# A cached-attention decode block on one core: the first and the last unit move into VectorE's and ScalarE's loops

## The chip, the core and the metric

The kernel runs on one core of one Trainium2 chip. The core has a matrix engine (TensorE, PE in the profile), a vector engine (VectorE, DVE), a scalar engine (ScalarE, ACT), GpSimd (POOL) and SyncE (SP), and 16 DMA engines that carry data between device memory and the on-chip memory. Each of the five engines runs its own list of instructions in order; they wait for one another through semaphores. In this kernel nearly all transfers are issued from SP, in one list and in order; ACT issues the first small input and the output.

The metric is device time in microseconds (us) of one execution. The kernel before takes 1277.06 us, the median of three runs (1276.95 to 1277.29).

## The reference, cut to what is computed

```python
B, Sq, D = 4, 1, 512
H, Sk, Dh = 32, 8192, 128
F = 1792

def _A_ref(x, k_cache, v_cache, wq, wo):
    q = (x @ wq).reshape(B, Sq, H, Dh).transpose(0, 2, 1, 3)
    scores = jnp.einsum("bhqd,bhkd->bhqk", q, k_cache) * (Dh ** -0.5)
    p = _softmax(scores, axis=-1)
    o = jnp.einsum("bhqk,bhkd->bhqd", p, v_cache)
    return o.transpose(0, 2, 1, 3).reshape(B, Sq, H * Dh) @ wo

def _B_ref(x, w_gate, w_up, w_down):
    return (_sigmoid(x @ w_gate) * (x @ w_up)) @ w_down

h = x + _A_ref(_layernorm(x), k_cache, v_cache, wq, wo)
return h + _B_ref(_layernorm(h), w_gate, w_up, w_down)
```

All inputs are bfloat16. The two caches are 4 x 32 x 8192 x 128 each, 268 MB each; the weights together are some 14 MB. One token per batch entry is decoded, so every cache byte is used once.

## The kernel before, in words

**Units.** The 128 pairs of batch entry and head are worked on four at a time: `NU` = 32 units. A unit has a K tile and a V tile, each 128 partitions x 64 KB (8 MB in all). The big tensor `KV` has `NSL` = 3 slots of that size: K of unit u goes to slot u % 2, V to slot 2 (the last V to slot 0). `KV` is declared at L172, after `kT`, `PTz`, `Lq`, `headw`, `q_all` (L170) and `spare` (L171; nothing reads or writes it), and its place in each partition follows from their sizes.

**The transfers** (L532 to L557, all on SP's list): Wq; then K0, K1, V0, K2, V1, K3 and so on in alternation (`order`); then Wo, Wgate, Wup and three pieces of Wdown. From the fourth tile on each K waits until unit u-2 has been read (`t_kd`, set by a small DVE memset at L361 behind the last transposition of a unit), and each V until the V tile before it has been used (`t_vd`, the first of four small matmuls at L415). V0 waits for the projection of q, which has read Wq out of slot 2.

**A unit** (`unit(u)`, L422) emits, in this order:
- `scores(u)`: 16 times, DVE transposes 128 x 1024 words of K into one half of `kT` (L335) and PE multiplies it with q (L344). `Lq` is a zeroed tensor in which `q_window(u)` (L328, DVE) puts the four queries of the unit, read from `q_all`.
- `maxima(u)`: DVE takes the row maximum (L361 to L367), ACT the exponential (L369).
- `q_window(u + 1)`, or in the last unit a memset of a dummy (L428).
- `pv(u - 1)`, not in unit 0: DVE's reciprocal of the sum of weights (L396), PE's 64 matmuls with V (L405), ACT's scaled copy to `O_sb` (L410; `O_sb` lies in the second half of `kT`), and the four small matmuls (L415), whose last token is `t_ex`.
- `weights(u)`: four DVE transpositions of the exponentials (L375), which wait for `t_ex` of the unit before, and a PE matmul that adds them up (L379, `t_sum`).

So DVE's order within a unit is 16 transpositions, the maxima, the next query window, the reciprocal, and the weights' transpositions.

**The lists and loops.** `_Prog` collects one list of steps for each engine. `open`, `begin`, `end` and `close` turn a part of a list into a loop on the chip: each turn is written out and must equal the first, and the loop runs it as often as there were turns. Semaphore counts go back to their start with each turn (`_rebase`, L67). Before, unit 0 is written out straight on all engines; PE then loops over units 1 to 31, one unit a turn; DVE and ACT loop over units 1 to 30, two units a turn (15 turns), and run unit 31 straight again. Behind the loop come twelve turns of `filler` matmuls on PE, `pv(31)`, the projection with Wo, the second layernorm and the gated unit, and the output.

Of the kernel before, what the change touches and what calls it, by code (L numbers as in the profile page):

```python
# [6 lines left out]
BF16 = mybir.dt.bfloat16  # L7
FP32 = mybir.dt.float32
ALU = mybir.AluOpType
# [9 lines left out]
class _Prog:  # L19
# [52 lines left out]
    def emit(self, eng, fn, waits=(), incs=1, ch=None):  # L72
        todo = self._waits(eng, waits)
        key = ch or eng
        tok = self.token(key, incs) if incs else None
        self._put(eng, todo, key, fn, incs, 1)
        return tok
# [41 lines left out]
def bass_sequential_preLN__mha_block_cached__glu_gated_glu__decode_kernel(  # L119
# [12 lines left out]
    B, _sq, D = A_x.shape  # L132
# [7 lines left out]
    NU = B * H // HU  # L140
# [4 lines left out]
    NT = R * DH // 2 // TW  # L145
# [8 lines left out]
    prog = _Prog({"p2d": "dve", "d2d": "dve", "a2d": "dve", "d2p": "pe", "a2p": "pe",  # L154
                  "d2a": "act", "p2a": "act",
                  "k0": "dve", "k1": "dve", "v2": "pe"})
    emit = prog.emit

    with ExitStack() as es:
        def SB(name, shape, dt):  # L160
            return es.enter_context(nc.sbuf_tensor(name, shape, dt))

        def raw(t):
            return t.tensor if hasattr(t, "tensor") else t
# [2 lines left out]
        PTz = SB("PTz", [128, 2048], BF16)  # L167
        Lq = SB("Lq", [128, 528], BF16)
        headw = SB("headw", [128, 128], FP32)
        q_all = SB("q_all", [128, NU, 4], BF16)  # L170
        spare = SB("spare", [128, 24], FP32)  # L171
        KV = SB("KV", [128, NSL * SLOT], BF16)  # L172
        E_sb = SB("E_sb", [128, 512], BF16)
# [3 lines left out]
        part = SB("part", [128, 32], FP32)  # L177
# [5 lines left out]
        dummy = SB("dumm", [128, 4], FP32)  # L183
# [32 lines left out]
        bank = [PS[:, 512 * i:512 * (i + 1)] for i in range(8)]  # L216
        SBK, OBK, EX, XS, XO, QB, DN = 0, 1, 2, 3, 4, (5, 6), 7
# [4 lines left out]
        for k in keys:  # L222
# [3 lines left out]
        slots = {(x, u): (0 if u == NU - 1 else 2) if x == "v" else u % 2 for x, u in order}  # L226
        toks = {x: prog.token(x[0] + str(slots[x]), 16) for x in order}
# [18 lines left out]
        t_mask = emit("pool", lambda e: e.affine_select(  # L246
            out=m42, in_=m42, compare_op=ALU.is_ge, fill=0.0, base=31,
            pattern=[[32, 4], [0, 2]], channel_multiplier=-1), [t0])
        t_lq0 = emit("pool", lambda e: e.memset(Lq[:, :], 0.0))
        t0 = emit("pool", lambda e: e.memset(lane[:, :], 0.0))  # L250
        for j in range(4):
# [9 lines left out]
        t_selc = emit("pool", lambda e: e.affine_select(  # L261
            out=hw4, in_=hw4, compare_op=ALU.is_ge, fill=0.0, base=31,
            pattern=[[0, 8], [32, 4], [0, 4]], channel_multiplier=-1), [t0])
        emit("pool", lambda e: e.memset(part[:, :], 1.0))
        t_pool = emit("pool", lambda e: e.memset(PTz[:, :], 0.0))
        for b in (OBK, EX, *QB, DN):
            t_ps0 = emit("act", lambda e, b=b: e.activation(bank[b], bass.AP(raw(Lq), 0, [[528, 128], [0, 512]]), ACT.Copy), [t_lq0])

        def cols(t, c):
            return t[:, c:c + NC * (B - 1) + 1:NC]  # L270
# [24 lines left out]
        for g in range(2):  # L295
            def f(e, g=g):
                made = []
                for c in range(NC):
                    for h in range(HU):
                        rhs = wq_v[:, c, 2048 * g:2048 * (g + 1)].rearrange("p (k h d) -> p h k d", k=4, h=HU)[:, h]  # L300
                        made.append(e.matmul(PS[32 * h:32 * h + B, 512 * QB[g]:512 * QB[g] + 512], cols(xnT, c), rhs,  # L301
                                             start=(c == 0), stop=(c == NC - 1), tile_position=(0, 32 * h)))
                return made[-4:]
# [3 lines left out]
            dst = qt[:, 512 * g:512 * (g + 1)].rearrange("p (k r w) -> p r k w", k=8, r=2)  # L307
            t_qr.append(emit("dve", lambda e, src=src, dst=dst: e.transpose(dst, src), [t_qp]))
        t_q = emit("dve", lambda e: e.tensor_copy(
            q_all[:, :, :].rearrange("p (b g) t -> p g b t", b=B),  # L310
            qt.rearrange("p (g t w) -> p g w t", t=4, g=NU // B)[:, :, 0:B, :]), t_qr)

        t_tr, t_sc, t_pv, t_ex, t_mx, t_exp, t_ptz, t_lq, t_ocp, t_rs, t_kd, t_vd, t_sum = ({} for _ in range(13))
        TU = 2
# [3 lines left out]
        def at(ix, d):  # L318
            return ix[d] if len(ix) > d else 0
# [5 lines left out]
        def q_window(u, t=0):  # L325
            dst = bass.AP(raw(Lq), 15, [[528, 128], [128, 4], [16, 8]])
            msk = bass.AP(raw(mask), 0, [[8, 128], [0, 4], [1, 8]])
            t_lq[u] = emit("dve", lambda e, ix: e.tensor_tensor(  # L328
                dst, bass.AP(raw(q_all), at(ix, 0) * (4 * TU) + 4 * (u - TU * t), [[NU * 4, 128], [1, 4], [0, 8]]), msk, ALU.mult),
                           [t_q, t_lq0, t_mask, t_sc.get((u - 1, NT - 1))], ch="d2p")  # L330

        def k_chunk(u, c):
            o = slots["k", u] * (SLOT // 2) + (NT - 1 - c) * TW
# [15 lines left out]
        def scores(u):  # L349
            clear(SBK, [t_lq[u], t_pool, t_ps0, t_selc])  # L350
            prog.open("pe")
            for c in range(NT):
                if c % 2 == 0:
                    prog.begin("pe")
                k_chunk(u, c)
                if c % 2:
                    prog.end("pe")
            prog.close("pe")
# [23 lines left out]
        def filler(n, turns=1):  # L382
            if turns > 1:
                prog.open("pe")
            for _ in range(turns):
                if turns > 1:
                    prog.begin("pe")
                emit("pe", lambda e: [e.matmul(bank[XS], Lq[:, 0:128], Lq[:, 0:512], start=True, stop=True) for _ in range(n)][-1],  # L388
                     [t_ps0, t_lq[NU - 1]], incs=0)
                if turns > 1:  # L390
                    prog.end("pe")
            if turns > 1:
                prog.close("pe")

        def pv(u, t):
            t_rs[u] = emit("dve", lambda e: e.reciprocal(rsb[:, :], bank[QB[1]][:, 1:2]), [t_sum[u]], ch="d2a")  # L396
            slot = slots["v", u]
            ob = 512 * OBK

            def f(e, ks):  # L400
                made = []
                for k in ks:
                    j, n, r4 = k % 4, k // 4, k % 4
                    lhsT = PTz[:, 512 * r4 + n:512 * r4 + n + 481:32]
                    made.append(e.matmul(PS[32 * j:32 * j + 16, ob:ob + 512], lhsT,  # L405
                                         KV[:, slot * SLOT + 512 * k:slot * SLOT + 512 * (k + 1)],
                                         start=(k < 4), stop=(k >= 60), tile_position=(0, 32 * j)))
                return made[-4:]
            t_pv[u] = emit("pe", lambda e: f(e, range(64)), [toks["v", u], t_ps0], incs=4, ch="p2a")
            t_ocp[u] = emit("act", lambda e: e.activation(O_sb, bank[OBK], ACT.Copy, scale=rsb[:, 0:1]), [t_pv[u], t_rs[u]], ch="a2p")  # L410

            def fs(e, ix, qs):
                ins = None
                for q in qs:
                    ins = e.matmul(bass.AP(raw(PS), at(ix, 0) * 4 + (512 * EX + 4 * (u - t)), [[4096, 128], [1, 4]]),  # L415
                                   O_sb[:, 128 * q:128 * (q + 1)], lane[:, q:q + 13:4],
                                   start=False, stop=(u == NU - 1 and q == 3), skip_group_check=True)
                return ins
            t_vd[u] = emit("pe", lambda e, ix: fs(e, ix, (0,)), [t_ocp[u], t_selc, t_ps0], ch="p2x")
            t_ex[u] = emit("pe", lambda e, ix: fs(e, ix, (1, 2, 3)), ch="p2d")  # L420

        def unit(u, t=0):  # L422
            scores(u)
            maxima(u)
            if u + 1 < NU:
                q_window(u + 1, t)
            else:
                emit("dve", lambda e: e.memset(dummy[:, 3:4], 0.0), ch="d2p")  # L428
            if u:
                pv(u - 1, u - 1)  # L430
            weights(u)

        emit("pe", lambda e: e.matmul(bank[EX][:, 0:128], PTz[:, 0:128], PTz[:, 0:128], start=True, stop=False,
                                      skip_group_check=True), [t_pool, t_ps0], incs=0)
        q_window(0)
        unit(0)

        prog.open("pe", "dve", "act")
        for u in range(1, NU):
            t, first = divmod(u - 1, TU)  # L440
            if u == NU - 1:
                prog.close("dve", "act")
                t = 0
            elif not first:
                prog.begin("dve", "act")
            prog.begin("pe")
            unit(u, t)
            prog.end("pe")
            if first:
                prog.end("dve", "act")  # L450
        prog.close("pe")
        filler(2, 12)
        pv(NU - 1, 0)
        t_oa = emit("dve", lambda e: e.tensor_tensor(  # L454
# [79 lines left out]
        for n, (x, u) in enumerate(order):  # L534
# [3 lines left out]
            slot = slots[x, u]  # L538
# [53 lines left out]
```

## Time and profile before

| | |
|---|---|
| median of three runs | 1277.06 us (1276.95 to 1277.29) |
| the profiled execution, its own time | 1276.83 us |
| its span, first to last instruction | 1275.6 us |
| busy: PE | 779.7 us |
| busy: DVE | 762.3 us |
| busy: ACT | 59.0 us |
| bytes moved by DMA | 550.83 MB |

The profile covers one execution. The span is what the trace covers; 1.2 us of the execution's own time lie outside it. Busy times are sums over an engine's instructions. The timeline's rows give the start from the span's beginning, the duration, the engine, the line of the kernel, the operation, what it writes and reads, and in brackets how long the engine was idle before and what ended that. A row for SPq or ACTq is the issue of a transfer; its landing shows in the instruction that waited for it. Queue rows count packets, megabytes and the time that the packets took as a share of the time of all 16 DMA engines.

### The profile page before, as it was taken

Reading aid. Unit: us, or ns where it says so; the run is one execution under the profiler, and the core shown is the slowest. Engines: PE = TensorE matmul, PEld = TensorE weight load, DVE = VectorE, ACT = ScalarE, POOL = GpSimd, SP = SyncE. Lnnn points to the kernel's source line nnn. Section 1 sums busy time; section 2 is a strip of 40 time slices with the busy share of each in tenths; the row PEclk is TensorE's granted clock in tenths of the full one; section 3 lists DMA queues with packets and bytes.
Section 4 is the critical chain, followed back from the end, with each engine's and each line's share of the span. In section 5 each row is a group of like instructions: output and inputs, shape, how many; then the busy total and the mean of one; then the engine's idle time right before and its main releaser. Section 6 shows DMA issues by size and latency. Waiting matters only on the chain.

```text
span 1275.6 us, 14073 instructions
## 1 busy us (share of the span) xinstructions
PE 779.7 (61%) x4588; PEld 328.5 (26%) x4636; DVE 762.3 (60%) x917; ACT 59.0 (5%) x114; POOL 5.7 (0%) x22
## 2 busy tenths in 40 slices
PE   1676755557755557655567655567555577555577
PEld 0232222223222223222222222222222232222233
DVE  1876665556665557665567655566655566655571
ACT  2000000000000000000000000000000000000001
POOL 1000000000000000000000000000000000000000
PEclk8888877788877788877788777788777888777888
DMA  9999999999999999999999999999999999999998
GB/s 423 432 426 430 427 450 434 430 430 427 454 430 430 430 427 454 432 427 430 430 452 432 427 430 434 450 430 427 430 440 444 430 427 430 442 442 430 430 427 371
DMA packets 10244, 550.83 MB, mean 432 GB/s; under 512 B 1144, under 2 KB 1152, under 8 KB 1408
## 3 DMA queue, kind: packets, MB, share of 16 engines
q1 hardware_dynamic: 10224, 550.77, 99.7%
q8 instruction: 2, 0.03, 0.0%
q10 hardware_dynamic: 16, 0.01, 0.0%
q14 instruction: 2, 0.02, 0.0%
HBM read 550.77 MB, written 0.00 MB: 432 GB/s over the span
## 4 chain that ended last, share of the span: by engine, by line
DMA 60%; PE 20%; DVE 12%; issue 2%; ACT 1%; SPq 0%; DVEq 0%
DMA KV<-in_A_k_cache_dram 58%; PE PS L344 14%; DVE kT L335 12%; PE PS L405 5%; DMA KV<-in_B_w_down_dram 3%; ACT kT L410 1%; PE PS L415 0%; SPq L541 0%; DVE PTz L375 0%; PE PS L521 0%; DVE KV L529 0%; SPq L557 0%; DVEq L112 0%
## 5 line engine op out<-in xcount | busy, mean ns | idle before, releaser
L344 PE MATMUL PS<-kT,Lq 128*128 128x512 bf16 x2048 | 588.7, 420 | 343.5 <-DVE kT L335 326.4
L335 DVE STREAM_TRANSPOSE kT<-KV 128x1024 f32<-128x1024 f32 x512 | 614.4, 1232 | 300.3 <-DMA KV<-in_A_k_cache_dram 237.5
L344 PEld LDWEIGHTS PS<-kT,Lq 128*128 x2048 | 210.3, 103 | 694.6 <-issue 621.7
L375 DVE STREAM_TRANSPOSE PTz<-E_sb 32x512 bf16<-32x512 bf16 x128 | 89.9, 703 | 129.1 <-PE PS L415 125.5
L405 PE MATMUL PS<-KV,PTz 128*16 128x512 bf16 x2048 | 117.0, 381 | 0.0
L379 PE MATMUL PS<-part,headw 128*128 128x2 f32 x64 | 18.8, 363 | 100.4 <-DVE PTz L375 100.4
L369 ACT ACTIVATE E_sb<-PS,negm 128x512 bf16<-128x512 f32 x32 | 22.0, 687 | 1139.4 <-DVE negm L367 1139.4
L405 PEld LDWEIGHTS PS<-KV,PTz 128*16 128x16 bf16 x2048 | 58.9, 111 | 56.3 <-issue 13.6
L415 PE MATMUL PS<-lane,kT 128*128 128x4 f32 x256 | 33.6, 255 | 31.0 <-ACT kT L410 31.0
L362 DVE TENSOR_REDUCE part<-PS 128x1 f32<-128x512 f32 x32 | 22.1, 691 | 38.7 <-PE PS L344 38.7
L415 PEld LDWEIGHTS PS<-lane,kT 128*128 128x128 f32 x256 | 31.0, 191 | 46.2 <-issue 44.8
L379 PEld LDWEIGHTS PS<-part,headw 128*128 128x128 f32 x64 | 16.0, 310 | 103.7 <-DVE PTz L375 103.7
L410 ACT ACTIVATE kT<-PS,rsb 128x512 f32<-128x512 f32 x32 | 22.0, 687 | 61.5 <-PE PS L405 61.5
L388 PE MATMUL PS<-Lq 128*128 128x512 bf16 x27 | 11.0, 462 | 2.9 <-issue 2.5
L328 DVE TENSOR_TENSOR Lq<-q_all,mask 128x32 bf16<-128x32 bf16 x32 | 9.5, 297 | 0.0
L454 DVE TENSOR_TENSOR kT<-PS,mask 128x512 bf16<-128x512 f32 x1 | 0.7, 692 | 13.3 <-PE PS L415 13.3
L367 DVE STREAM_TRANSPOSE negm<-mxr 128x32 f32<-128x32 f32 x32 | 6.8, 212 | 1.1
L364 DVE STREAM_TRANSPOSE turn<-part 128x32 f32<-128x32 f32 x32 | 6.8, 211 | 1.1
L388 PEld LDWEIGHTS PS<-Lq 128*128 128x128 bf16 x44 | 4.8, 116 | 8.3 <-issue 6.1
L322 PEld LDWEIGHTS PS<-Lq,headw 128*128 128x128 bf16 x32 | 3.5, 108 | 12.8 <-issue 11.3
L396 DVE RECIPROCAL rsb<-PS 128x1 f32<-128x1 f32 x32 | 6.3, 197 | 0.7 <-PE PS L379 0.7
L301 PE MATMUL PS<-KV,kT 128*4 128x512 bf16 x32 | 3.6, 627 | 5.0 <-DMA KV<-in_A_wq_dram 5.0
(70 smaller groups left out, 56.7 us busy)
## 6 DMA issues: line engine op xcount, KB each, us to landing
KV<-in_A_wq_dram SPq DMA_DIRECT2D x1, 4096.0 KB, 12.2
KV<-in_A_wo_dram SPq DMA_DIRECT2D x1, 4096.0 KB, 27.2
KV<-in_B_w_gate_dram SPq DMA_DIRECT2D x1, 1792.0 KB, 31.1
KV<-in_B_w_up_dram SPq DMA_DIRECT2D x1, 1792.0 KB, 34.9
KV<-in_B_w_down_dram SPq DMA_DIRECT2D x1, 1024.0 KB, 32.1
KV<-in_A_k_cache_dram SPq DMA_DIRECT2D x32, 49.6
KV<-in_A_v_cache_dram SPq DMA_DIRECT2D x32, 30.7
KV<-in_B_w_down_dram SPq DMA_DIRECT2D x1, 512.0 KB, 32.9
```

The lines of the kernel that those rows point to most:

```text
L328: t_lq[u] = emit("dve", lambda e, ix: e.tensor_tensor(dst, bass.AP(raw(q_all), at(ix, 0) * (4 * TU) + 4 * (u - TU * t), [[NU * 4, 128], [1 ...
L335: t_tr[u, c] = emit("dve", lambda e: e.transpose(kT[:, (c % 2) * TW:(c % 2 + 1) * TW], KVw[:, o:o + TW]), w, ch="d2p")
L344: ins = e.matmul(bank[SBK], bass.AP(raw(Lq), ix[-1] * 2 + (128 * t + c % 2), [[528, 128], [1, 128]]), rhs, start=False, stop=False, skip_g ...
L362: a = emit("dve", lambda e: e.tensor_reduce(part[:, 0:1], bank[SBK], AX.X, ALU.max), [t_sc[u, NT - 1], t_pool], ch="d2d")
L364: a = emit("dve", lambda e: e.transpose(turn_[:, :], part[:, :]), [a], ch="d2d")
L369: t_exp[u] = emit("act", lambda e: e.activation(E_sb[:, :], bank[SBK], ACT.Exp, bias=negm[:, 0:1], scale=SCALE, accum_out=part[:, 1:2]), [ ...
L375: return [e.transpose(PTz[32 * q:32 * (q + 1), :].rearrange("p (r q c) -> p r q c", r=4, q=4)[:, :, q, :], E_sb[32 * q:32 * (q + 1), :].re ...
L379: t_sum[u] = emit("pe", lambda e: e.matmul(bank[QB[1]][:, 0:2], headw[:, :], part[:, 0:2], start=True, stop=True), [t_ptz[u], t_selc], ch= ...
L388: emit("pe", lambda e: [e.matmul(bank[XS], Lq[:, 0:128], Lq[:, 0:512], start=True, stop=True) for _ in range(n)][-1], [t_ps0, t_lq[NU - 1] ...
L405: made.append(e.matmul(PS[32 * j:32 * j + 16, ob:ob + 512], lhsT, KV[:, slot * SLOT + 512 * k:slot * SLOT + 512 * (k + 1)], start=(k < 4), ...
L410: t_ocp[u] = emit("act", lambda e: e.activation(O_sb, bank[OBK], ACT.Copy, scale=rsb[:, 0:1]), [t_pv[u], t_rs[u]], ch="a2p")
L415: ins = e.matmul(bass.AP(raw(PS), at(ix, 0) * 4 + (512 * EX + 4 * (u - t)), [[4096, 128], [1, 4]]), O_sb[:, 128 * q:128 * (q + 1)], lane[: ...
```

## The change

```diff
-        q_all = SB("q_all", [128, NU, 4], BF16)
+        q_all = SB("q_all", [128, NU + 1, 4], BF16)
...
         emit("pool", lambda e: e.memset(part[:, :], 1.0))
+        emit("pool", lambda e: e.memset(q_all[:, NU, :], 0.0))
         t_pool = emit("pool", lambda e: e.memset(PTz[:, :], 0.0))
...
-            q_all[:, :, :].rearrange("p (b g) t -> p g b t", b=B),
+            q_all[:, 0:NU, :].rearrange("p (b g) t -> p g b t", b=B),
...
-                           [t_q, t_lq0, t_mask, t_sc.get((u - 1, NT - 1))], ch="d2p")
+                           [t_q, t_lq0, t_mask, t_pool, t_sc.get((u - 1, NT - 1))], ch="d2p")
...
-                     [t_ps0, t_lq[NU - 1]], incs=0)
+                     [t_ps0, t_lq[NU]], incs=0)
...
-            slot = slots["v", u]
+            slot = slots.get(("v", u))
...
-            t_pv[u] = emit("pe", lambda e: f(e, range(64)), [toks["v", u], t_ps0], incs=4, ch="p2a")
+            if u < 0:
+                t_pv[u] = prog.token("p2a", 4)
+                prog._put("pe", [], "p2a", lambda e: e.nop(), 1, 4)
+            else:
+                t_pv[u] = emit("pe", lambda e: f(e, range(64)), [toks["v", u], t_ps0], incs=4, ch="p2a")
             t_ocp[u] = emit("act", lambda e: e.activation(O_sb, bank[OBK], ACT.Copy, scale=rsb[:, 0:1]), [t_pv[u], t_rs[u]], ch="a2p")
+
+            if u < 0:
+                t_ex[u] = emit("pe", lambda e: e.nop(), [t_ocp[u]], ch="p2d")
+                return
...
             scores(u)
             maxima(u)
-            if u + 1 < NU:
-                q_window(u + 1, t)
-            else:
-                emit("dve", lambda e: e.memset(dummy[:, 3:4], 0.0), ch="d2p")
-            if u:
-                pv(u - 1, u - 1)
+            q_window(u + 1, t)
+            pv(u - 1, u - 1)
             weights(u)
...
         q_window(0)
-        unit(0)
-
-        prog.open("pe", "dve", "act")
-        for u in range(1, NU):
-            t, first = divmod(u - 1, TU)
-            if u == NU - 1:
-                prog.close("dve", "act")
-                t = 0
-            elif not first:
+        t_sum[-1] = emit("pe", lambda e: e.matmul(bank[QB[1]][:, 0:2], headw[:, :], part[:, 0:2], start=True, stop=True),
+                         [t_q, t_pool, t_selc], ch="p2d")
+
+        prog.open("dve", "act")
+        for u in range(NU):
+            t, odd = divmod(u, TU)
+            if u == 1:
+                prog.open("pe")
+            if not odd:
                 prog.begin("dve", "act")
-            prog.begin("pe")
+            if u:
+                prog.begin("pe")
             unit(u, t)
-            prog.end("pe")
-            if first:
+            if u:
+                prog.end("pe")
+            if odd:
                 prog.end("dve", "act")
-        prog.close("pe")
+        prog.close("pe", "dve", "act")
```

DVE's and ACT's loops now run over units 0 to 31 in 16 turns of two units, so that unit 0 and unit 31 are no longer written out beside them; DVE's list holds 94 steps instead of 153, ACT's 37 instead of 42. PE keeps its form: unit 0 straight, then 31 turns.

A loop's turns must be equal, so unit 0 gets the steps that the other units have for the unit before, with nothing behind them: a matmul that gives a sum of ones (`t_sum[-1]`), DVE's reciprocal of it, a PE nop in place of the 64 matmuls with V, ACT's copy of the zeroed bank to `O_sb`, and a second PE nop in place of the four small matmuls, on which unit 0's `weights` now wait. Unit 31 gets a query window for a unit 32 that doesn't exist; `q_all` is one unit longer for it (8 more bytes in each partition), and GpSimd sets that part to zero. The fillers behind the loop then multiply with that zero window.

More of the change, by code (lines that the diff above doesn't have):

```diff
@@ L328, in q_window @@
             t_lq[u] = emit("dve", lambda e, ix: e.tensor_tensor(
-                dst, bass.AP(raw(q_all), at(ix, 0) * (4 * TU) + 4 * (u - TU * t), [[NU * 4, 128], [1, 4], [0, 8]]), msk, ALU.mult),
-                           [t_q, t_lq0, t_mask, t_sc.get((u - 1, NT - 1))], ch="d2p")
+                dst, bass.AP(raw(q_all), at(ix, 0) * (4 * TU) + 4 * (u - TU * t), [[(NU + 1) * 4, 128], [1, 4], [0, 8]]), msk, ALU.mult),
+                           [t_q, t_lq0, t_mask, t_pool, t_sc.get((u - 1, NT - 1))], ch="d2p")
         def k_chunk(u, c):
```

## The prediction

> **What bounds the kernel now.** I read the page first: the span, the slices of DMA, the queues, the chain of work.
>
> ```profile
> span 1275.6 us, 14073 instructions
> DMA  9999999999999999999999999999999999999998
> q1 hardware_dynamic: 10224, 550.77, 99.7%
> q8 instruction: 2, 0.03, 0.0%
> q14 instruction: 2, 0.02, 0.0%
> HBM read 550.77 MB, written 0.00 MB: 432 GB/s over the span
> DMA 60%; PE 20%; DVE 12%; issue 2%; ACT 1%; SPq 0%; DVEq 0%
> ```
>
> The 16 DMA engines are full in every slice, so the 40% of the chain that is not DMA is compute during which other transfers run. Two rows for K tiles late in the timeline, and the queue over most of the span, show the pace:
>
> ```profile
> 1173.46 2.37 DVE L335 STREAM_TRANSPOSE kT<-KV 128x1024 f32<-128x1024 f32 x2 [7.78 <-DMA KV<-in_A_k_cache_dram]
> 1201.05 0.81 SPq L541 DMA_DIRECT2D KV<-in_A_v_cache_dram  x2
> 1212.12 2.37 DVE L335 STREAM_TRANSPOSE kT<-KV 128x1024 f32<-128x1024 f32 x2 [7.42 <-DMA KV<-in_A_k_cache_dram]
> ...
> DMA packets 8194, 477.24 MB, mean 434 GB/s; under 512 B 912, under 2 KB 912, under 8 KB 912
> q1 hardware_dynamic: 8194, 477.24, 100.1%
> ```
>
> From one K tile to the next pass 38.66 us, two tiles of 8.39 MB: 434 GB/s, the rate of the whole stretch from 100 to 1200 us. VectorE waits over 7 us for each K tile, and a V tile is issued 11 us before the K tile in flight has landed. In the steady state a unit may thus be 7 us longer before anything moves. 550.83 MB at 434 GB/s are 1269.2 us; what stands around them is the start and the end.
>
> ```profile
> 0.80 0.57 ACTq L235 DMA_DIRECT2D KV<-in_A_x_dram  x1
> 2.41 0.68 DVE L273 BATCH_NORM_STATS2 kT<-KV 4x6 f32<-4x512 bf16 x1 [2.41 <-DMA KV<-in_A_x_dram]
> 32.27 2.37 DVE L335 STREAM_TRANSPOSE kT<-KV 128x1024 f32<-128x1024 f32 x2 [14.21 <-DMA KV<-in_A_k_cache_dram]
> 91.74 2.37 DVE L335 STREAM_TRANSPOSE kT<-KV 128x1024 f32<-128x1024 f32 x2 [1.21 <-DMA KV<-in_A_k_cache_dram]
> 1251.61 3.65 PE L405 MATMUL PS<-KV,PTz 128*16 128x512 bf16 x64
> 1255.40 0.69 ACT L410 ACTIVATE kT<-PS,rsb 128x512 f32<-128x512 f32 x1 [16.53 <-PE PS L405]
> 1257.23 0.69 DVE L454 TENSOR_TENSOR kT<-PS,mask 128x512 bf16<-128x512 f32 x1 [13.29 <-PE PS L415]
> 1271.63 2.15 PE L521 MATMUL PS<-KV 128*4 128x256 bf16 x28 [0.68 <-DMA KV<-in_B_w_down_dram]
> 1273.39 0.09 PEld L521 LDWEIGHTS PS<-KV 128*4 128x4 bf16 x4 [0.33 <-DMA KV<-in_B_w_down_dram]
> ```
>
> A transfer issued at 0.80 has landed by 2.41, so 1.6 us pass before bytes arrive; the last piece of Wdown is taken at 1273.39, 2.2 us before the end. 1.6 + 1269.2 + 2.2 = 1273.0, and 2.6 us of the span remain. More than half of them lie in one place: K0 lands at 32.27, K2 at 91.74, three tiles later, which at 19.33 each would be 57.99 us and are 59.47: 1.48 us lost. In that stretch lie the only two instruction fetches of the first 1200 us; these rows are of the windows from 63 to 64 and from 87 to 88 us:
>
> ```profile
> q14 instruction: 1, 0.01, 1.9%
> q8 instruction: 1, 0.02, 5.8%
> ```
>
> Of 16 engines for 1 us these shares are 0.30 and 0.93 us. The larger one (16 KB) comes while TensorE, the engine with the longest list, is in its first turn; the smaller (8 KB) belongs to one of the short lists.
>
> **The change part by part.** Nothing is taken from the transfers: SP's list keeps its issues, its order and its waits, and no queue is passed by anything.
>
> *Unit 0's empty steps.* These are the rows of unit 0's end and of unit 1's:
>
> ```profile
> 56.00 0.69 ACT L369 ACTIVATE E_sb<-PS,negm 128x512 bf16<-128x512 f32 x1 [47.73 <-DVE negm L367]
> 56.58 0.19 ACT L369 ACTIVATION_READ_ACCUMULATOR E_sb<-PS,negm 128x1 f32 x1
> 56.81 2.91 DVE L375 STREAM_TRANSPOSE PTz<-E_sb 32x512 bf16<-32x512 bf16 x4 [0.67 <-ACT E_sb L369]
> 59.75 2.37 DVE L335 STREAM_TRANSPOSE kT<-KV 128x1024 f32<-128x1024 f32 x2
> 85.63 0.69 ACT L410 ACTIVATE kT<-PS,rsb 128x512 f32<-128x512 f32 x1 [1.45 <-PE PS L405]
> 86.47 1.05 PE L415 MATMUL PS<-lane,kT 128*128 128x4 f32 x8 [0.97 <-ACT kT L410]
> 86.88 0.33 SPq L541 DMA_DIRECT2D KV<-in_A_v_cache_dram  x1
> 87.63 2.90 DVE L375 STREAM_TRANSPOSE PTz<-E_sb 32x512 bf16<-32x512 bf16 x4 [4.05 <-PE PS L415]
> ```
>
> Unit 0's weights start at 56.81, as soon as ACT has its sum (56.77). Now ACT's copy comes in between: 0.69 us by the row at 85.63, 0.15 from its end (86.32) to PE's start, 0.1 for the nop (an estimate: no nop is in the trace), 0.11 from PE's end (87.52) to VectorE. Sum 1.05 us. The reciprocal stands before the exponential is over and costs nothing. Behind the weights on VectorE is all of unit 1, which had K1 waiting, so unit 1 moves by 1.05 us, and V1's issue from 86.88 to 87.93. It is late only if the engines run dry: K2 lands at 91.74 and an issue needs 1.6 us, so there are 3.3 us, of which 1.05 are used. Unit 1's weights end at 90.53 + 1.05 = 91.58, still ahead of K2. The cost is 0. Bounds: 0 as long as the delay is under 3.3 us, and from there on 1 us for each us.
>
> *The loops' ends.* A turn's end now lies behind the odd unit instead of the even one. Behind unit 1 it meets the 1.21 us of idle time at 91.74, now 0.16; if it takes 0.5 us, unit 2 starts 0.3 us late and the next K tile is 38 us away: 0. Later turns have 7 us. The exits come ahead of `pv(31)`, when ACT has 16.53 us of idle time before 1255.40 and VectorE 13.29 before 1257.23: 0.
>
> *Unit 31* in the loop:
>
> ```profile
> 1197.46 0.30 DVE L328 TENSOR_TENSOR Lq<-q_all,mask 128x32 bf16<-128x32 bf16 x1
> 1235.87 0.06 DVE L428 MEMSET dumm<- 128x1 f32 x1
> 1240.18 2.90 DVE L375 STREAM_TRANSPOSE PTz<-E_sb 32x512 bf16<-32x512 bf16 x4 [4.17 <-PE PS L415]
> 6.99 1.28 ACT L369 ACT_TABLE_LOAD   x1
> ```
>
> A window of 0.30 us replaces a memset of 0.06, and 4.17 us of idle time follow: 0. ACT's table for the exponential, loaded once at 6.99, may have to be loaded at the head of each of the 16 turns; its 1.28 us stand where ACT waits for a unit's maxima (47.73 us in unit 0): 0. The extra sum, GpSimd's memset and the wait on `t_pool` fall into VectorE's 14.21 us before K0: 0. The fillers multiply zeros now; should that slow the tail, Wdown covers 0.68 us at 1271.63.
>
> *Shorter lists.* VectorE loses 59 of 153 steps, so the 8 KB fetch may be gone. The 1.48 us are of both fetches; shared out by size, a third, 0.5 us, is the small one's. If the two hit different DMA engines, the longer alone sets the pace of tiles that are spread over all 16, and the gain is nothing. Bounds 0 and 1.48; between, I take 0.3.
>
> *`q_all` grows by 8 bytes.* This is the one part that touches every transfer. `KV` follows `q_all` and `spare`, and in the compiled program of before it begins at byte 30,720 of each partition, 120 x 256. Tensors there start at multiples of 32, so it moves to 30,752, and all rows land 32 bytes beyond a multiple of 256. No transfer of before lands like that, so this is bounded by rows. Below: nothing. Above: the landing is cut once more, like a new row. The window from 1262 to 1271 us, with rows of 8 and 14 KB, tells what a row costs:
>
> ```profile
> DMA packets 471, 3.74 MB, mean 415 GB/s; under 512 B 56, under 2 KB 56, under 8 KB 190
> q1 hardware_dynamic: 471, 3.74, 98.0%
> ```
>
> 3.74 MB at 434 GB/s are 8.62 us and took 9.00: 0.38 us for 415 rows (471 less 56 tiny packets) on 16 engines, 15 ns each; without the 2% in which the queue was idle 0.20 us, 8 ns. An engine carries 568 rows (512 of the caches, 56 of the weights), so one more start for each costs 4.5 to 8.5 us. The low end is one more piece of 32 bytes in a row: at 27.1 GB/s for an engine 1.2 ns, 0.7 us in all. I take that, since a row of 65,536 bytes moved by 32 differs only at its two ends. [...]
>
> **The sum.** The profiled execution took 1276.83 us (span 1275.6, 1.2 outside). -0.3 for the fetch, +0.7 for the landing, 0 for the rest: 1277.2. That execution was 0.23 below the median of the runs, so against the median 1277.5.
>
> **The rivals.**
>
> *Row starts decide (slower).* The moved landing costs a whole start for each row: +4.5 to 8.5 us, less the fetch: 1281 to 1285. For it: every byte passes there and DMA has no slack at all. Against it: there are as many rows as before. It decides from 4.5 ns a row on (2.55 us).
>
> *Every stretch off its boundary pays.* The rows run like the weights' short ones, 415 instead of 434 GB/s: 550.83 MB take 1327.3 us instead of 1269.2, +58: 1335. For it: the rate of before lies within 1% of the best in any stretch, with all rows on a boundary, so nothing shows what they do off it. Against: nothing but that a landing's pieces other than the ends are whole.
>
> *V1 runs dry.* If unit 0's empty steps cost 5 us instead of 1.05, the engines stand for 1.7 us: 1278.8. Against: all the rows summed are short.
>
> [...]
>
> *Only the fetch counts.* The landing costs nothing and the fetch its upper end: 1275.6.
>
> **How the numbers follow.** Forecast, 1277.5 with its own range 1275.8 to 1279.6: 0.55. Row starts: 0.18. Every stretch: 0.15. V1: 0.04. Fetch each turn: 0.03. Fetch only: 0.05. I leave out the every-stretch case and part of the fetch in each turn, under 0.2: the range is 1275.6 to 1283. About 0.2% (2.55 us) is what a measurement of this kernel can tell from no change. Faster than that would need 1274.5, beyond the 1.48 us that any part could give back: 0.02. Slower: row starts, every stretch, fetch in each turn and a part of V1 and of the forecast's upper end, 0.41. Within: 0.57.
>
> **What would show it.** K tiles late in the run 38.66 to 38.70 us apart show that the landing costs what I took; 38.8 or more shows row starts, 40 us the every-stretch case. K0 to K2: 59.5 us, or 59.0 if the fetch's cost is gone; the queue of instruction packets shows one or none on q14. Unit 0's weights should start near 57.9, V1's issue near 87.9, with K2 at its old place. Wdown's last piece at 1273 to 1274. I would be wrong if the packets of 64 KB take longer, or if DMA's slices show a hole.

## The result, and the profile after

| | before | after |
|---|---|---|
| median | 1276.95 us (1276.62 to 1277.37, 15 runs) | 1279.79 us (1279.39 to 1280.99, 15 runs) |
| ratio, 95% interval | | 1.0024 [1.0017, 1.0031] |
| the profiled execution, its own time | 1276.83 us | 1280.04 us |
| its span | 1275.6 us | 1278.8 us |

The kernel became slower by 2.84 us. The forecast, no measurable change at 1277.5, was 2.3 us short; the time lies in the range, 0.2 us above the forecast's own upper end of 1279.6. The page of after, span, slices of DMA and queues first, then the new group among the costliest ones:

```profile
span 1278.8 us, 14108 instructions
DMA  9999999999999999999999999999999999999998
q1 hardware_dynamic: 10224, 550.77, 99.7%
q8 instruction: 2, 0.03, 0.0%
q14 instruction: 2, 0.02, 0.0%
...
L370 ACT ACT_TABLE_LOAD x16 | 20.5, 1283 | 0.3
```

The same packets and bytes pass, DMA is as full as before in every slice, and the code is fetched as often as before: two packets on each instruction queue. The engines have not run out of transfers anywhere; so the transfers must have become longer. The timeline of after gives the places, by the K tiles that VectorE takes and the last piece of Wdown:

```profile
32.36 2.37 DVE L336 STREAM_TRANSPOSE kT<-KV 128x1024 f32<-128x1024 f32 x2 [14.27 <-DMA KV<-in_A_k_cache_dram]
91.98 2.37 DVE L336 STREAM_TRANSPOSE kT<-KV 128x1024 f32<-128x1024 f32 x2 [0.18 <-DMA KV<-in_A_k_cache_dram]
130.70 2.37 DVE L336 STREAM_TRANSPOSE kT<-KV 128x1024 f32<-128x1024 f32 x2 [7.86 <-DMA KV<-in_A_k_cache_dram]
1176.14 2.37 DVE L336 STREAM_TRANSPOSE kT<-KV 128x1024 f32<-128x1024 f32 x2 [8.25 <-DMA KV<-in_A_k_cache_dram]
1214.86 2.37 DVE L336 STREAM_TRANSPOSE kT<-KV 128x1024 f32<-128x1024 f32 x2 [7.61 <-DMA KV<-in_A_k_cache_dram]
1276.59 0.09 PEld L528 LDWEIGHTS PS<-KV 128*4 128x4 bf16 x4 [0.34 <-DMA KV<-in_B_w_down_dram]
```

K2 comes 0.24 us later than before (91.98 against 91.74), K31 2.74 us later (1214.86 against 1212.12), the last piece of Wdown 3.20 us later (1276.59 against 1273.39), which is the whole 3.2 us of the span. Between K2 and K31 lie 58 tiles, 1122.88 us instead of 1120.38. The 2.50 us are no event at one place: spread over 58 tiles they are on average 0.043 us a tile, and with 8 rows of a tile on each DMA engine 5.4 ns a row. One pair of tiles alone shows little: 38.72 us from 1176.14 to 1214.86, against 38.66. VectorE's idle time ahead of each K tile from K3 on is still 7.4 to 8.3 us, against 7.2 to 8.2 before, so compute has nothing to do with it.

The windows of after in which the first fetches lie, and the timeline around units 0 and 1:

```profile
q14 instruction: 1, 0.01, 1.9%
...
q8 instruction: 1, 0.02, 6.6%
```

```profile
56.45 0.69 ACT L370 ACTIVATE E_sb<-PS,negm 128x512 bf16<-128x512 f32 x1 [48.19 <-DVE negm L368]
57.04 0.19 ACT L370 ACTIVATION_READ_ACCUMULATOR E_sb<-PS,negm 128x1 f32 x1
57.13 0.68 ACT L415 ACTIVATE kT<-PS,rsb 128x512 f32<-128x512 f32 x1
58.01 2.90 DVE L376 STREAM_TRANSPOSE PTz<-E_sb 32x512 bf16<-32x512 bf16 x4 [1.37 <-PEq L418]
...
87.60 1.28 ACT L370 ACT_TABLE_LOAD   x1
88.15 0.33 SPq L548 DMA_DIRECT2D KV<-in_A_v_cache_dram  x1
```

The first is of 67 to 68 us, the second of 87 to 88: the small fetch has moved by 4.8 us (63.12 to 67.93 us in the trace's records of single packets) and is not gone. The empty copy stands ahead of unit 0's weights, which start 0.78 us after the exponential's sum is over (58.01 against 57.23) instead of 0.04. V1 is issued at 88.15 instead of 86.88. The exponential itself came 0.45 us later than before (56.45 against 56.00); the first experiment has the same steps and its copy 0.57 us earlier, so this part is not theirs. Over the profiled executions of all kernels it begins anywhere from 55.86 to 56.77.

### The profile page after: what moved, and what is told of

Read it like the earlier page. It is cut to its first block, busy times and chain, and to the rows that moved or that the text cites. A ratio compares the mean times of both kernels' runs of the same rounds, so it can differ in the third digit from the quotient of the medians.

```text
span 1278.8 us, 14108 instructions
## 1 busy us (share of the span) xinstructions
PE 779.2 (61%) x4590; PEld 328.3 (26%) x4638; DVE 762.4 (60%) x918; ACT 78.8 (6%) x130; POOL 5.8 (0%) x23
```

## The experiments

Two theories stood against each other. Landing: `KV` has moved 32 bytes off a multiple of 256, and every row pays for it. Steps: the new instructions, the loops' ends or the late V1 cost the time. `spare` lies between `q_all` and `KV` and nothing uses it, so its size changes no step: it moves `KV` and the small tensors behind it. A row here is the 64 KB that a tile's transfer brings to one partition; each DMA engine carries 8 of them for a tile (the 64 tiles are 8192 packets of 64 KB on 16 engines).

**The change with `KV` put back on a multiple of 256.**

```diff
         q_all = SB("q_all", [128, NU + 1, 4], BF16)
-        spare = SB("spare", [128, 24], FP32)
+        spare = SB("spare", [128, 16], FP32)
```

> The kernel after, with spare cut from 24 to 16 words, so that KV begins at byte 30,720 again, a multiple of 256; all steps of the change are in it. Landing theory (the 2.8 us come from rows that land 32 bytes off a multiple of 256): the loss goes, 1276.6 to 1277.3 us, late tiles 19.32 us apart as before. Step theory (they come from the empty steps of unit 0, the later issue of V1, the 16 table loads or the moved instruction fetches): the loss stays, 1279.4 to 1280.2 us, late tiles 19.36 us apart.

Measured: 1277.11 us, 1.0002 [0.9993, 1.0011] of before (ten of the eleven runs took up to 1277.47, one 1278.85). Its page and its timeline:

```profile
q14 instruction: 2, 0.02, 0.0%
...
L370 ACT ACT_TABLE_LOAD x16 | 20.5, 1283 | 0.3
```

```profile
56.56 0.68 ACT L415 ACTIVATE kT<-PS,rsb 128x512 f32<-128x512 f32 x1
57.43 1.43 DVE L376 STREAM_TRANSPOSE PTz<-E_sb 32x512 bf16<-32x512 bf16 x2 [1.37 <-PEq L418]
...
87.01 0.33 SPq L548 DMA_DIRECT2D KV<-in_A_v_cache_dram  x1
91.65 2.37 DVE L336 STREAM_TRANSPOSE kT<-KV 128x1024 f32<-128x1024 f32 x2 [0.99 <-DMA KV<-in_A_k_cache_dram]
...
1173.45 2.37 DVE L336 STREAM_TRANSPOSE kT<-KV 128x1024 f32<-128x1024 f32 x2 [7.97 <-DMA KV<-in_A_k_cache_dram]
1212.11 2.37 DVE L336 STREAM_TRANSPOSE kT<-KV 128x1024 f32<-128x1024 f32 x2 [7.42 <-DMA KV<-in_A_k_cache_dram]
```

All steps of the change are there: the empty copy, the 16 table loads, the longer turns, the shorter lists. K31 comes at 1212.11, before at 1212.12. The steps together cost nothing that can be measured (1277.11 us against 1277.05), and they give nothing.

**Only the move: before, with `KV` 32, 64 and 128 bytes further.**

```diff
-        spare = SB("spare", [128, 24], FP32)
+        spare = SB("spare", [128, 32], FP32)
```

(40 and 56 words for 64 and 128 bytes.)

> The kernel before, with spare grown from 24 to 32 words, so that KV and all behind it lie 32 bytes further; no step is changed. Landing theory: slower by 2 to 3 us, 1279 to 1280 us, late tiles 19.36 us apart. Step theory: no change, 1276.6 to 1277.4 us, 19.32 us.

> The kernel before with spare grown from 24 to 40 words: KV at 30,784, 64 bytes beyond a multiple of 256. If any place off a multiple of 256 costs: 1278.9 to 1280 us, between or beside the moves by 32 (1279.7) and by 128 (1279.1). If the cost fell with the piece that is cut off and 64 were a whole line: 1277 us.

> The kernel before, with spare grown from 24 to 56 words: KV and all behind it 128 bytes further, 30,848, half way between two multiples of 256. Landing theory, if any place off a multiple of 256 costs the same: 1279 to 1280 us. Landing theory, if only the odd 32 bytes of a 64- or 128-byte line count: 1276.6 to 1277.4 us. Step theory: 1276.6 to 1277.4 us.

| `KV` begins at | time | ratio to before |
|---|---|---|
| 30,752 (32 off) | 1279.70 us | 1.0022 [1.0012, 1.0031] |
| 30,784 (64 off) | 1279.15 us | 1.0016 [1.0007, 1.0025] |
| 30,848 (128 off) | 1279.14 us | 1.0017 [1.0008, 1.0026] |

The timeline of the kernel moved by 32 bytes:

```profile
32.52 2.37 DVE L335 STREAM_TRANSPOSE kT<-KV 128x1024 f32<-128x1024 f32 x2 [14.27 <-DMA KV<-in_A_k_cache_dram]
91.83 2.37 DVE L335 STREAM_TRANSPOSE kT<-KV 128x1024 f32<-128x1024 f32 x2 [0.88 <-DMA KV<-in_A_k_cache_dram]
130.55 2.37 DVE L335 STREAM_TRANSPOSE kT<-KV 128x1024 f32<-128x1024 f32 x2 [7.93 <-DMA KV<-in_A_k_cache_dram]
...
1214.69 2.37 DVE L335 STREAM_TRANSPOSE kT<-KV 128x1024 f32<-128x1024 f32 x2 [7.79 <-DMA KV<-in_A_k_cache_dram]
```

The move alone makes 2.65 us (1279.70 less 1277.05) of the change's 2.84; the two moved kernels' own medians lie 0.09 us apart. From K2 to K31 it takes 1122.86 us, in after 1122.88. Over the 568 rows of an engine 2.65 us are 4.7 ns a row. Going from 32 to 128 bytes off makes it no dearer. It is even a little cheaper: at 64 and 128 bytes no run took more than 1279.41 us, at 32 none less than 1279.54. Why is open. One oddity: K0 to K2 takes 59.31 us, not more than before (59.47). The cost starts later, of which more below.

**The control: 32 bytes behind `KV`, which stays; and `KV` on an odd multiple of 256.**

```diff
         KV = SB("KV", [128, NSL * SLOT], BF16)
+        spare2 = SB("spare2", [128, 8], FP32)
         E_sb = SB("E_sb", [128, 512], BF16)
```

```diff
-        q_all = SB("q_all", [128, NU, 4], BF16)
         spare = SB("spare", [128, 24], FP32)
         KV = SB("KV", [128, NSL * SLOT], BF16)
+        q_all = SB("q_all", [128, NU, 4], BF16)
```

> The kernel before, with 8 unused words between KV and E_sb: KV stays at 30,720, only the small tensors behind it lie 32 bytes further. Landing theory: no change, 1276.6 to 1277.4 us. If it is the engines' small operands that pay for the move: up to 1279.8 us. Step theory: no change.

> The kernel before with q_all declared behind KV, so that KV begins at byte 30,464, 119 x 256: a multiple of 256 but not of 512. If multiples of 256 are what counts: 1276.6 to 1277.4 us, no change. If the place must be a multiple of 512 or more, or if any move from 30,720 costs: 1279 to 1280 us.

Measured: 1277.02 us for both, 1.0000 [0.9991, 1.0009] and 1.0000 [0.9991, 1.0009]. So it is not the place of the small tensors behind `KV` that counts, and an odd multiple of 256 costs nothing either: at 30,464, which is 119 x 256, the time is that of 120 x 256 (1277.02 us against 1277.00).

**By the row or by the byte: each tile in two transfers of 32 KB rows, on 256 and 32 bytes off.** The bytes stay, the rows double. If the move costs by the row, it costs twice as much here; if by the byte, the same.

```diff
-        toks = {x: prog.token(x[0] + str(slots[x]), 16) for x in order}
+        toks = {x: prog.token(x[0] + str(slots[x]), 32) for x in order}
...
-            prog.dma("sp", f"{x}{slot}", lambda e, src=src, slot=slot: e.dma_start(reg(slot, 0, SLOT), src), [w],
-                     tok=toks[x, u])
+            for a in (0, SLOT // 2):
+                prog.dma("sp", f"{x}{slot}", lambda e, src=src, slot=slot, a=a: e.dma_start(
+                    reg(slot, a, SLOT // 2), src[:, a:a + SLOT // 2]), [w], tok=toks[x, u])
```

> The kernel before with each K and V tile fetched by two transfers of half a row, 32 KB, on the same semaphore; the same bytes land at the same place, in 1024 rows for each DMA engine instead of 512. By the row start of 8 ns that the prediction read from the weights: 512 x 8 ns = 4.1 us more, 1281.2 us; by its 15 ns 7.7 us more, 1284.7 us; if a row's start costs nothing, 1277 us. (SP's list is longer by 64 issues, which may add an instruction fetch, up to 1 us.)

> The same halves, with KV 32 bytes further (spare 32 words). Against halves_on_256: if the move costs by the row, twice what it cost whole rows, 2 x 2.65 = 5.3 us (4.5 to 6); if it costs by the byte or by the tile, once, 2.65 us (2 to 3.2).

Measured: 1279.98 us on 256 (1.0024 [1.0015, 1.0033]) and 1285.98 us 32 off (1.0072 [1.0058, 1.0086], five runs from 1285.31 to 1287.77). The K31 rows of the first kernel and of the second:

```profile
1215.10 2.37 DVE L335 STREAM_TRANSPOSE kT<-KV 128x1024 f32<-128x1024 f32 x2 [7.88 <-DMA KV<-in_A_k_cache_dram]
```

```profile
1220.38 2.37 DVE L335 STREAM_TRANSPOSE kT<-KV 128x1024 f32<-128x1024 f32 x2 [7.53 <-DMA KV<-in_A_k_cache_dram]
```

The move puts K31 off by 5.28 us with half rows (1220.38 less 1215.10) and by 2.57 with whole ones (1214.69 less 1212.12): twice as much for twice the rows. The transfers doubled with the rows; what tells the two apart is the packet records, in which each 32 KB row takes 1217.9 ns instead of 1213.0 (means from 450 to 1200 us). The cost goes by the row. Over the whole run it is 6.00 us for 1080 rows, 5.6 ns each. The first kernel by itself prices a row's start: 512 more rows on each engine (and twice as many transfers) for 2.98 us, 5.8 ns each, where I expected 8. A row that lands off a multiple of 256 thus costs nearly as much as one row more.

This pair also told whose the second small fetch is. The window from 706 to 707 us of the first kernel, and that from 1207 to 1208 us of before, hold the same row:

```profile
q14 instruction: 1, 0.01, 1.9%
```

```profile
q14 instruction: 1, 0.01, 1.9%
```

The only list that became longer is SP's, by 64 issues, and the fetch came 500 us earlier. So it is taken to be SP's, and a shorter list on VectorE can't remove it.

**How late may V1 be? Unit 0's weights behind 3 and 8 more copies on ScalarE,** in the kernel before, with `KV` on its multiple.

```diff
+            if u == 0:
+                late = None
+                for _ in range(3):
+                    late = emit("act", lambda e: e.activation(O_sb, bank[OBK], ACT.Copy), [late])
+                t_late.append(late)
...
-            t_ptz[u] = emit("dve", f, [t_exp[u], t_pool, t_ex.get(u - 1)], incs=4, ch="d2p")
+            t_ptz[u] = emit("dve", f, [t_exp[u], t_pool, t_ex.get(u - 1), t_late[0] if u == 0 else None], incs=4, ch="d2p")
```

> The kernel before, with three extra copies of 0.69 us on ScalarE, each waiting for the one before, between unit 0's exponential and its weights (about 0.8 us each with the wait, 2.5 us; the change itself put in 1.2 us). The prediction's cover of 3.3 us for V1's issue: nothing is lost, 1276.6 to 1277.4 us, weights of unit 0 at about 59.3 us, V1's issue at about 89.4 us. If the cover was smaller than worked out: up to 2.5 us more, 1279.5 us.

> The same with eight copies: unit 0's weights and V1's issue about 6.6 us late, V1's issue at about 93.5 us. With a cover of 3.3 us and 1 us for each us beyond it: 3.3 us lost, 1280.3 us, and a hole in the transfers around 92 to 95 us. If a late V1 costs nothing at all (the tiles behind it catch up): 1277 us.

Measured: 1278.61 us with 3 copies (1.0013 [1.0004, 1.0022], 1.50 us more than before; runs from 1277.42 to 1279.92) and 1281.39 with 8 (1.0033 [1.0021, 1.0046], 4.28 us more). The copies take 0.62 us each, back to back, so V1 was less late than expected and cost more. The timeline of before at K3, then of the kernel with 3 and of that with 8 copies from unit 0's end to K3:

```profile
130.35 2.37 DVE L335 STREAM_TRANSPOSE kT<-KV 128x1024 f32<-128x1024 f32 x2 [7.37 <-DMA KV<-in_A_k_cache_dram]
```

```profile
57.01 1.84 ACT L376 ACTIVATE kT<-PS 128x512 f32<-128x512 f32 x3
58.96 2.91 DVE L381 STREAM_TRANSPOSE PTz<-E_sb 32x512 bf16<-32x512 bf16 x4 [2.49 <-ACT kT L376]
88.82 0.33 SPq L547 DMA_DIRECT2D KV<-in_A_v_cache_dram  x1
131.30 2.37 DVE L336 STREAM_TRANSPOSE kT<-KV 128x1024 f32<-128x1024 f32 x2 [8.16 <-DMA KV<-in_A_k_cache_dram]
```

```profile
56.54 4.99 ACT L376 ACTIVATE kT<-PS 128x512 f32<-128x512 f32 x8
61.63 2.91 DVE L381 STREAM_TRANSPOSE PTz<-E_sb 32x512 bf16<-32x512 bf16 x4 [5.63 <-ACT kT L376]
92.00 0.33 SPq L547 DMA_DIRECT2D KV<-in_A_v_cache_dram  x1
133.10 2.37 DVE L336 STREAM_TRANSPOSE kT<-KV 128x1024 f32<-128x1024 f32 x2 [6.54 <-DMA KV<-in_A_k_cache_dram]
```

V1 issued 1.94 us later than before (88.82 against 86.88) puts K3 off by 0.95 us, 5.12 us later by 2.75; the rest of the loss shows up in the tiles behind. The cover is therefore smaller than the 3.3 us of the prediction, under 1.94. The packet records (no view of the profile) say why: the 16 engines don't end a tile together. In before the first of them has ended K2's rows at 89.55 us, the middle one at 89.75, the last at 91.26; VectorE's start at 91.74 shows the last one alone. The first engine begins with V1 0.95 us after its issue (88.82 to 89.78, and 92.00 to 92.95), so with an issue after 88.6 the first engines stand: 1.7 us later than in before. With 8 copies the engines stood from 89.5 to 90.4 until 92.95 to 94.12, the hole that was expected. The first row of V1 is then slow as well, 2.97 us (3 copies) and 3.14 (8 copies) at the median instead of 2.42.

The rows become slow before any engine stands. In after V1 is issued at 88.15, no engine had a gap, and yet the first row of V1 took 2.47 to 3.00 us on 14 of the 16, 2.71 at the median of all. The empty steps are not needed for it: in the kernel moved by 128 bytes, where the exponential came late by itself, V1 is issued at 88.10, and the median is 2.54:

```profile
88.10 0.33 SPq L541 DMA_DIRECT2D KV<-in_A_v_cache_dram  x1
```

In after this cost nothing that can be seen. The engine that ends K2 last, at 91.50, took 2.42 us over its first row of V1, and from K2 to K3 pass 38.72 us (91.98 to 130.70), as in before moved by 32 bytes (91.83 to 130.55), where V1 is issued at 87.30.

**What the packet records say of the moved rows.** No view of the profile gives the duration of one row, so these are means over the trace's records of 64 KB packets, and the spacing of the tiles in them (tiles counted from 0):

| kernel | first two tiles, ns a row | tiles 20 to 63, ns a row | us a tile, tiles 15 to 63 |
|---|---|---|---|
| before | 2419.3 | 2418.1 | 19.319 |
| after | 2419.1 | 2422.7 | 19.360 |
| moved by 32 | 2419.3 | 2422.7 | 19.360 |
| moved by 64 | | 2421.9 | 19.353 |
| moved by 128 | | 2421.8 | 19.351 |
| after, back on 256 | | 2418.1 | 19.320 |

A row off the multiple takes 4.6 ns longer, which is the 4.7 ns of the total time. But in the first two tiles it takes no longer, in after as in before moved by 32 bytes (2419.1 and 2419.3 ns against 2419.3), and then single engines turn slower, in after the early ones only for some tiles (tiles 7 and 8 take 2444.4 and 2430.5 ns a row over all engines, tiles 9 to 11 again 2418.1 to 2418.5); from tile 13 on all 16 are slower to the end (2422.5 ns in tile 13 of after), in after and in before moved by 32 bytes alike. The two engines whose rows an instruction fetch has just delayed are among the first (4.4 and 4.5 ns a row more than 2418 in tile 5 of after). That the engines get out of step and then pay for the odd landing would fit, but no run tested it; it stays open.

## Why the prediction was right or wrong

**What bounds the kernel: right.** DMA is busy nine tenths or more in 39 of 40 slices of both kernels and eight in the last, the slack of 7 us and more at each K tile stayed, and only what touches the transfers moved the time.

**The moved landing: the step that failed, by its size.** "`q_all` grows by 8 bytes" was named as the one part that touches every transfer, and K tiles further apart were to show it. I took 1.2 ns a row, 0.7 us, "since a row of 65,536 bytes moved by 32 differs only at its two ends". That it costs by the row was right (the halves show it). The price was wrong: 4.7 ns a row, 2.65 us. I priced the odd end by its 32 bytes at an engine's rate; the upper bound's price, a row's start (8 ns there, 5.8 measured with the halves), was the nearer one. By its own point, 4.5 ns a row, the rival "row starts decide" was to take over, and at 4.7 it just did, though the time stayed below its 1281 us: its mechanism is nearer to what was measured than the forecast's. Of the signs named ahead, late K tiles 38.72 us apart fell between the two values set (up to 38.70 for the forecast, 38.8 for row starts), and the sign of being wrong came true: the 64 KB packets take longer, 2422.7 ns instead of 2418.1. That a row pays for an odd end by its bytes was an estimate, and no run shows it; the runs show 4.7 ns, four times the 1.2 that I took, and 128 bytes off no dearer than 32 (1279.14 us against 1279.70). They show too that a start off 256 costs (2.09 us at 128 bytes to 2.65 at 32, with 2.15 at 64) and that 119 x 256 does not (1277.02 us).

**The fetch: wrong, 0 instead of 0.3 us of gain.** The number of fetches stayed; one small fetch only moved, the other is taken to be SP's (it came 500 us earlier with 64 more issues there). The argument that stood beside the forecast would have been enough: by before's packet records the small fetch delays one DMA engine by about 0.8 us (its next row begins 0.30 us late and takes 2.95 us instead of 2.42) and the large one another by 1.4 us (0.90 us, and 2.93), and tiles spread over all 16 wait for the longer delay (K2's last row ends at 91.26 us, the middle engine's at 89.75, and VectorE starts at 91.74). The two hit different engines, as the lower bound supposed. That removing the small one would give nothing is argued; no run removed it.

**Unit 0's empty steps: right that they cost nothing, but not for the reason given.** The delay is 0.74 us (0.78 less 0.04) instead of 1.05, since the copy begins before the read of the accumulator is over (57.13 against 57.23). The cover of 3.3 us was taken from the landing on the slowest engine; the first engine stands from an issue 1.7 us later than in before on, and in after, 1.27 us later (0.45 of it from the late exponential), the first rows of V1 were already slow on 14 of 16 engines. That this stayed free is in part luck: the last engine, which sets the pace, was behind the others by what the instruction fetch had cost it (its next row began 1.03 us late and took 2.93 us). The rival "V1 runs dry" fell for this change, yet its point of decision was too far out, and its loss doesn't start at nothing where the engines begin to stand, since the slow first rows come on top.

**Loops' ends, unit 31, the zeros in the fillers, the extra sum: right, 0.** The kernel with all of them and `KV` on its multiple takes what before takes (1277.11 us against 1277.05). The 16 table loads came as foreseen, 1.28 us each, and are hidden.

**The other rivals fell.** "Every stretch" wanted 40 us from K tile to K tile, there are 38.72. A fetch in each of the 16 turns would show on the instruction queues, which have two packets each in both kernels. "Only the fetch counts" fell with the fetch.

**The chances.** Row starts had 0.18 and the forecast 0.55. The time is in the range only because the range took in part of the rival's outcomes; it is 0.2 us above the forecast's own upper end. Between two bounds of 0.7 and 8.5 us I gave the low end three times the weight of the high one, on an argument about the ends of a row that no row of the trace priced; the measured 2.65 us lies between them.

No kernel faster than before was found. The change with `KV` on a multiple of 256 takes the same time as before, with the shorter lists.

## What to carry to other kernels

Where DMA is the bound, an edit to the size of a small tensor is an edit to all tensors behind it: look at where the big transfers land, and keep them on a multiple of 256 bytes (here 119 x 256 and 120 x 256 took the same time, and 32 bytes off cost 0.2%, more than every instruction that the change added). Price a cost by the row by what a row's start costs (5.8 ns here, for the 4.7 that the move cost), not by the odd bytes (1.2 ns). To judge how late a transfer may be issued, count from when the first DMA engine ends its share of the one before, not from when the whole tile has landed. Here an issue 1.3 to 1.4 us ahead of that end (88.15 ahead of 89.42, 88.10 ahead of 89.52) already had slow first rows, one 1.9 us ahead (87.49 ahead of 89.42, moved by 64 bytes) had not.

## What the runs showed of the hardware that was not expected

- Rows of 64 KB that landed off a multiple of 256 bytes took 2422.7 ns (32 bytes off) or 2421.8 to 2421.9 (64 and 128 bytes off) instead of 2418.1, but not from the first tile on: single engines turned slower first, and only from tile 13 on (32 bytes off) were all of them slower (why is open).
- The first 64 KB row of V1, issued late, took longer than 2.42 us: 2.71 us at the median with no gap before it (after), 2.97 and 3.14 with 3 and 8 copies, where engines stood.
- The first and the last of 16 engines end one tile 1.7 us apart (89.55 and 91.26 us), of 19.3 us that a tile takes; the last is the one that the larger instruction fetch delayed by 1.4 us, and it stays last to the end (tile 63 ends at 1249.0 us on the middle engine and at 1250.39 on the last).
